# Order of a partial product, a GELU and two loads in the first two waves of an attention and MLP kernel

## The chip, the cores and the metric

The kernel runs on one core of a Trainium2 chip. The metric is the device time of one execution in microseconds; the median of several runs counts. Engines: PE (TensorE, matrix products), PEld (its weight loads), DVE (VectorE), ACT (ScalarE), POOL (GpSimd), and SP (SyncE), which here issues DMAs.

## The reference

The reference is a linear attention with decay per head, followed by an MLP with the quick GELU. Cut to what matters:

```python
q, k, v: (4, 8, 768, 64)   # batch, heads, sequence, head size; lam: (8,)
for b in range(12):                       # blocks of 64 positions
    intra = (qb @ kb.T) * Dmask           # lam ** (i - j) below the diagonal
    out[block] = intra @ vb + (qb * lam_pow) @ kv_state
    kv_state = lam**64 * kv_state + (kb * rev_pow).T @ vb
x = out as (3072 tokens, 512)
h = x @ w_in                              # 512 x 2048
y = (h * sigmoid(1.702 * h)) @ w_out      # 2048 x 512, result in float32
```

## The kernel before

The 3072 tokens are worked in six waves (0 to 5) of 512 tokens. Waves 0 and 1 take two batches each over 256 positions, in two halves c; waves 2 to 5 take 128 positions of all four batches. For each wave the kernel loads q, k and v, casts k and q to bf16 with their decay factors (`do_cast`), transposes them (`turn_pe` on PE, or `turn_dma` as a DMA transpose from SP, L248), multiplies scores (`d_scores` L262, `n_scores` L338), masks them, multiplies with v and the state, and writes the attention's result to `xT`. The MLP follows.

Products of both MLP layers are mostly made by a Strassen-like scheme of seven products on half blocks, numbered 1 to 7. Each product runs into a bank of PSUM (X, Q, V, in the first wave also W); some are copied out as a `part`, others are added to a part (`h_sb`, L604; `o_sb`, L488, L531). Products 5, 6, 7 and 3 use sums of the left side, products 4 to 7 differences of weights. The differences are made on DVE: `w_in_t` (L564) and `w_out_t` (`weight_sums`, L431), the sums `g_s` at L444, `x_s` at L577.

The tile framework runs in manual schedule: each engine executes its instructions in the order in which the code writes them, and semaphores are set from data and buffers. The order is hand written. For waves 1 to 5 it is a string of short steps (`STEPS`), each run by `one_step`: `a6` is product 6 of the first group of the first layer (with the copy or eviction of its bank; `v` at the end puts the copy on DVE, otherwise it is ACT, L224), `A5` the GELU behind product 5 of that group (`in_gelu`, L615), with b/B, c/C for the other groups; `P20` is product 2 of the second layer, half 0 (L464); `S`, `M`, `m` are scores and masks of the next wave, `v0` and `v1` the casts of v for it on ACT, `R` the rest of its attention; `gl`, `gh` are sums of the GELU's output, `L` loads, `i` differences of `w_in`, `X` the sums of x. The second wave (wave 1) has a head that is written out call by call ahead of `STEPS[1]`.

The second layer of wave 0 is `product0(n, m0, m1)`: steps m0 to m1 of the eight along the inner dimension of product n, for both halves of the tokens (two matmuls for each step). The weights `w_out` come in four chunks of four, so steps 0 to 2 use chunk 0, and 6 to 8 use chunk 3. POOL issues the loads of `w_in` and `w_out`; SP issues all loads of q, k and v but one, all DMA transposes and all stores. `leave0` evicts wave 0's banks; the stores wait in `late` and are issued where they are called.

Loads of wave 2 are split: `load(2, "kq")` stands in wave 0, `load(2, "v")` in the head of wave 1, between the two pairs of transposes of wave 2. `gate_pool` (L682) makes POOL wait for a sum of x before it casts the second k and q of wave 2. Stores, loads and transposes share SP's queue, in order. The tile of v has one buffer for each half.

Of the kernel before, what the change touches and what calls it, by code (L numbers as in the profile page):

```python
# [25 lines left out]
def kernel(  # L26
# [52 lines left out]
    def load_one(w, c, nm, src):  # L79
        x = ld.tile([P, H, 2 * D], f32, tag=f"{nm}{c}", bufs=LD_BUFS[nm], name=f"{nm}f")  # L80
        if w < ND:
            n = H if w or (nm == "v" and c) else H // 2
            for h in range(0, H, n):
                (nc.gpsimd if w == 0 and c and nm == "v" else nc.sync).dma_start(
                    out=x[:, h : h + n],
                    in_=src[2 * w + c, h : h + n, 0 : 2 * P, :].rearrange("h (s a) d -> s h (a d)", a=2))
        else:
            nc.sync.dma_start(out=x.rearrange("p h (a d) -> p (h a) d", a=2),
                              in_=src[2 * c : 2 * c + 2, :, w * P : (w + 1) * P, :].rearrange("b h s d -> s (b h) d"))
        loaded[w, c, nm] = x  # L90

    def load(w, nms="kqv"):
        src = {"k": k, "q": q, "v": v}
        if w < ND:
            for c in range(HF):
                for nm in nms:
                    if w or c == 0 or nm != "v":
                        load_one(w, c, nm, src[nm])
        else:
            for nm in nms:  # L100
                for c in range(HF):
                    load_one(w, c, nm, src[nm])
# [37 lines left out]
    def acc(name, dt=f32, shape=None, tag="a"):  # L140
        return ps.tile(shape or [P, 4, P], dt, tag=tag, bufs={"a": 5, "mm": 3}[tag], name=name)
# [104 lines left out]
    def turn_dma(w, c, nm):  # L246
        y = work.tile([P, 2 * NP, P], bf16, tag=f"{nm}T{c}", bufs={"k": 1, "q": 2}[nm], name=f"{nm}T")
        nc.sync.dma_start_transpose(out=y, in_=cast[w, c, nm].rearrange("p b c -> p (b c)"))  # L248
        trans[w, c, nm] = y
# [149 lines left out]
    def mlp1(w, fc):  # L399
        if w not in g_of:  # L400
            g_of[w] = gp.tile([P, FFC, W], bf16, tag="g", name="g_sb")
        j, i = w_in_of[fc]
        h = acc("ps_h", shape=[P, W], tag="mm")
        for kc in range(KC):
            nc.tensor.matmul(h, w_in_sb[j][:, kc, i * P : (i + 1) * P], xT[w][:, kc, :],
                             start=(kc == 0), stop=(kc == KC - 1))
        nc.scalar.activation(g_of[w][:, fc, :], h, GELU)
# [25 lines left out]
    def token_half(w, i, kh):  # L433
        return g_of[w].rearrange("p (m two) (i t) -> p two i m t", two=2, i=2)[:, kh, i]
# [11 lines left out]
    def w_half(m, kh, c):  # L446
        return w_out_sb[2 * m // CW][:, (2 * m) % CW + kh, c * 256 : (c + 1) * 256]
# [55 lines left out]
    def product0(n, m0, m1):  # L503
        if m0 == 0 and n in (1, 2, 7, 4):
            blocks[0, BANK0[n]] = acc(f"ps_{BANK0[n]}", shape=[P, 2, 256], tag="a" if n == 4 else "mm")
        bank = blocks[0, BANK0[n]]
        raw = [[token_half(0, i, kh) for kh in range(2)] for i in range(2)]
        x = {1: raw[0][0], 2: raw[0][1], 4: raw[1][1]}
        x = x[n] if n in x else half_sum[0][{5: 0, 6: 1, 7: 2, 3: 3}[n]]
        for t in range(2):  # L510
            for m in range(m0, m1):
                y = {1: (0, 0), 2: (1, 0), 3: (1, 1)}.get(n)
                y = w_half(m, *y) if y else TS[{4: 3, 5: 0, 6: 1, 7: 2}[n]][:, m]
                nc.tensor.matmul(bank[:, t], x[:, m, t * P : (t + 1) * P], y,  # L514
                                 start=(n in (1, 2, 7, 4) and t == 0 and m == 0),
                                 stop=(m == FFC // 2 - 1), skip_group_check=True)
# [62 lines left out]
    def in_product(w, g, n, tag, copy):  # L579
        if w not in g_of:  # L580
            g_of[w] = gp.tile([P, FFC, W], bf16, tag="g", name="g_sb")
        if isinstance(tag, dict):
            if n in (1, 2, 7):
                c = CHAIN[n]
                h_bank[w, g, c] = acc(f"ps_h{c}", shape=[P, 2, 256], tag=tag[c])
        elif n == 1:
            for c in tag[1:]:
                h_bank[w, g, c] = acc(f"ps_h{c}", shape=[P, 2, 256], tag={"a": "a", "m": "mm"}[tag[0]])
        bank, sums = h_bank[w, g, CHAIN[n]], x_sum.get(w)
        y = {1: (0, 0), 2: (0, 1), 4: (1, 1)}.get(n)  # L590
        y = x_half(w, *y) if y else sums[{5: 0, 6: 1, 7: 2, 3: 3}[n]]
        b = {1: (0, 0), 2: (1, 0), 3: (1, 1)}.get(n)
        for u in range(2):
            z = in_half(g, *b, u) if b else TI[g][{5: 0, 6: 1, 7: 2, 4: 3}[n]][:, :, u]
            for kc in range(2):
                nc.tensor.matmul(bank[:, u], z[:, kc], y[:, kc],  # L596
                                 start=(n in (1, 2, 7) and u + kc == 0), stop=(kc == 1), skip_group_check=True)
        if n in (1, 6, 7):
            h_part[w, g, n] = p = op.tile([P, 2, 256], f32, tag="part", bufs=6, name="part")
            copy(p, bank)  # L600
            return
        if n != 3:
            h = op.tile([P, 2, 256], f32, tag="o", name="h_sb")
            nc.vector.tensor_tensor(h, h_part[w, g, {2: 1, 5: 7, 4: 6}[n]], bank, op=ADD)  # L604
            bank = h
        if n == 3:
            in_gelu(w, g, n, bank)
        else:
            h_out[w, g, n] = bank
# [8 lines left out]
    def one_step(w, s):  # L618
        if s[0] == "+":
            w, s = w + 1, s[1:]  # L620
        x, a = w + 1, s[1:]
        if s[0] == "f":
            mlp1(w, int(a))
        elif s[0] in "abcd":
            k = "abcd".index(s[0])
            in_product(w, GR[w][k], int(s[1]), TAGS[w][k], dve_copy if s[2:] == "v" else act_copy)
        elif s[0] in "ABCD":
            in_gelu(w, GR[w]["ABCD".index(s[0])], int(a))
        elif s[0] == "i":
            in_sums(0, (int(a),))  # L630
        elif s[0] == "P":
            product(w, int(s[1]), (int(s[2]),))
        elif s[0] in "kq":
            do_cast(x, int(a), s[0], nc.vector)
        elif s[0] in "KQ":
            do_cast(x, int(a), s[0].lower(), nc.gpsimd)
        elif s[0] == "t":
            turn_dma(x, int(s[2]), s[1])
        elif s[0] == "v":
            cast_v(x, int(s[1]), ((act_copy, dve_copy)[s[2:] == "v"],))  # L640
        elif s[0] == "S":
            n_scores(x, int(a))
        elif s[0] == "M":
            n_masks(x, int(a))
        elif s[0] == "m":
            n_masks(x, int(a), True)
        elif s[0] == "R":
            n_rest(x)
        elif s[0] == "o":
            c11.pop(w)()  # L650
        elif s[0] == "X":
            x_sums(x)
        elif s[0] == "G":
            gate_pool(x_sum[w][3][0:1, 0, 0:1])
        elif s[0] == "g":
            m0, m1 = {"l": (0, 4), "h": (4, 8)}[s[1]]
            g_sums(w, m0, m1, tuple(int(c) - 1 for c in s[2:]))
        elif s[0] == "L":
            load(w + (1 if a == "w" else 2), "kq" if a == "k" else "v")
        else:  # L660
            raise ValueError(s)

    STEPS = {
# [17 lines left out]
    def gate_pool(x):  # L681
        nc.gpsimd.tensor_copy(behind_q, x)  # L682
# [4 lines left out]
    with tc.manual_schedule():  # L687
# [104 lines left out]
        product0(2, 4, 6)  # L792
        product0(4, 0, 4)
        product0(7, 4, 6)
        for n in (1, 2, 7):
            product0(n, 6, 8)
            if n != 2:
                leave0(n)
# [4 lines left out]
        cast_v(1, 0, (pool_copy, pool_copy))  # L803
        for nm in "kq":
            do_cast(1, 1, nm, nc.gpsimd)
        product0(4, 4, 8)
        leave0(4)
        leave0(2)
        turn_pe(1, 0, "k")
# [32 lines left out]
        for s in "A2 a7v c1".split():  # L842
            one_step(1, s)
        mlp1_half(1, 1, 4, 13)
        one_step(1, "B2")
        late[2]()
        late[5]()
        for nm in "kq":
            turn_dma(2, 0, nm)
        load(2, "v")  # L850
        gate_pool(x_sum[1][3][0:1, 0, 0:1])
        for nm in "kq":
            do_cast(2, 1, nm, nc.gpsimd)
            turn_dma(2, 1, nm)
        late[3]()
        late[4]()
        for s in STEPS[1].split():
# [34 lines left out]
```

## Time and profile before

| what | value |
|---|---|
| median of 3 runs | 194.1 us (193.7 to 194.93) |
| profiled execution, time | 194.76 us |
| profiled execution, span | 193.0 us |
| PE busy | 184.1 us, 95% of the span |
| DVE, ACT, POOL busy | 154.5, 130.2, 54.1 us |
| granted TensorE clock | 0.999 |
| HBM read and written | 27.26 and 6.29 MB |

The page of the profile gives busy times of one execution. The span starts with the first instruction and ends with the last; the execution's own time is 1.76 us more than the span. Times of single instructions come from the timeline of an engine: the start in us from the span's start, the duration, engine, line, operation, output and inputs, shapes, count, and in brackets the idle time before it with what ended that. Matmuls overlap, so for PE the distance between starts is the cost, not the duration shown: four matmuls of 128x256 start 0.44 us after the four before them.

### The profile page before, as it was taken

Reading aid. Unit: us, or ns where it says so; the run is one execution under the profiler, and the core shown is the slowest. Engines: PE = TensorE matmul, PEld = TensorE weight load, DVE = VectorE, ACT = ScalarE, POOL = GpSimd, SP = SyncE. Lnnn points to the kernel's source line nnn. Section 1 sums busy time; section 2 is a strip of 40 time slices with the busy share of each in tenths; the row PEclk is TensorE's granted clock in tenths of the full one; section 3 lists DMA queues with packets and bytes.
Section 4 is the critical chain, followed back from the end, with each engine's and each line's share of the span. In section 5 each row is a group of like instructions: output and inputs, shape, how many; then the busy total and the mean of one; then the engine's idle time right before and its main releaser. Section 6 shows DMA issues by size and latency. Waiting matters only on the chain.

```text
span 193.0 us, 5556 instructions
## 1 busy us (share of the span) xinstructions
PE 184.1 (95%) x2293; PEld 150.8 (78%) x2293; DVE 154.5 (80%) x296; ACT 130.2 (67%) x243; POOL 54.1 (28%) x79
## 2 busy tenths in 40 slices
PE   7689999899999899999999999999999999999993
PEld 2357646788787688888888888888888888888882
DVE  1796699877696899888799979799879797889950
ACT  4867664155868956469878388878388876597711
POOL 5488300039727000097000195000393000000000
PEclk9999999999999999999999999999999999999999
DMA  5999999999998989967799836999365903300113
GB/s 152 307 251 184 200 207 206 279 294 292 237 160 199 215 195 233 225 163 112 159 239 225 257 109 153 203 256 242 132 163 115 212 7 109 112 3 0 49 35 137
DMA packets 89599, 33.91 MB, mean 176 GB/s; under 512 B 67430, under 2 KB 89446, under 8 KB 89574
## 3 DMA queue, kind: packets, MB, share of 16 engines
q1 hardware_dynamic: 84676, 28.84, 61.6%
q0 software_dynamic: 4896, 4.72, 14.5%
q8 instruction: 18, 0.29, 0.7%
q14 instruction: 7, 0.06, 0.1%
q10 hardware_dynamic: 2, 0.00, 0.0%
HBM read 27.26 MB, written 6.29 MB: 174 GB/s over the span
## 4 chain that ended last, share of the span: by engine, by line
PE 72%; DMA 16%; POOL 5%; SPq 2%; DVE 2%; issue 0%; ACT 0%; POOLq 0%; DVEq 0%; ACTq 0%
PE ps_X L464 18%; PE ps_hX L596 15%; PE ps_V L464 9%; DMA w_out<-in_moe_w_out_dram 9%; PE ps_hV L596 7%; PE ps_Q L464 5%; PE ps_hQ L596 4%; DMA vf<-in_v_dram 3%; PE ps_X L514 3%; DMA qf<-in_q_dram 3%; PE ps_s L338 2%; PE ps_o L393 2%; DMA qT<-qs 2%; SPq L248 1%; POOL w_in L184 1%; PE ps_o L380 1%
## 5 line engine op out<-in xcount | busy, mean ns | idle before, releaser
L615 ACT ACTIVATE g_sb<-h_sb 128x512 bf16<-128x512 f32 x57 | 34.5, 631 | 1.7 <-DVE h_sb L604 1.7
L464 PEld LDWEIGHTS <-g_s 128*128 128x128 bf16 x320 | 30.9, 98 | 4.1
L596 PEld LDWEIGHTS <-w_in_t 128*128 128x128 bf16 x304 | 29.7, 98 | 4.1 <-issue 0.5
L224 ACT COPY part<-ps_hX 128x512 f32<-128x512 f32 x34 | 19.5, 587 | 10.5 <-PE ps_hX L596 10.3
L464 PEld LDWEIGHTS <-g_sb 128*128 128x128 bf16 x240 | 22.8, 98 | 3.4
L596 PEld LDWEIGHTS <-w_in 128*128 128x128 bf16 x228 | 22.1, 98 | 2.8
L596 PE MATMUL ps_hX<-x_s,w_in_t 128*128 128x256 bf16 x152 | 22.6, 272 | 0.4 <-ACT part L224 0.4
L444 DVE TENSOR_TENSOR g_s<-g_sb 128x1024 bf16<-128x1024 bf16 (+1 forms) x26 | 16.5, 646 | 5.6 <-ACT g_sb L615 5.6
L464 PE MATMUL ps_X<-w_out_t,g_s 128*128 128x256 bf16 x160 | 19.1, 273 | 0.0
L682 POOL CAST behind_q<-x_s 1x1 f32<-1x1 bf16 x4 | 0.7, 176 | 63.7 <-DVE x_s L577 63.7
L212 POOL TENSOR_TENSOR qs<-qf,q_pow 128x512 bf16<-128x512 f32 x16 | 16.3, 1041 | 1.1 <-DMA qf<-in_q_dram 1.1
L604 DVE TENSOR_TENSOR h_sb<-part,ps_hX 128x512 f32<-128x512 f32 x19 | 12.9, 681 | 4.5 <-PE ps_hX L596 4.5
L212 POOL TENSOR_TENSOR ks<-kf,k_pow 128x512 bf16<-128x512 f32 x16 | 16.3, 1040 | 0.1
L221 DVE COPY part<-ps_hV 128x512 f32<-128x512 f32 x18 | 12.4, 687 | 3.2 <-PE ps_hV L596 3.2
L604 DVE TENSOR_TENSOR h_sb<-part,ps_hV 128x512 f32<-128x512 f32 x19 | 13.0, 683 | 1.0 <-PE ps_hV L596 1.0
L604 DVE TENSOR_TENSOR h_sb<-part,ps_hQ 128x512 f32<-128x512 f32 x19 | 12.9, 680 | 0.4 <-PE ps_hQ L596 0.4
L615 ACT ACTIVATE g_sb<-ps_hX 128x512 bf16<-128x512 f32 x19 | 11.1, 589 | 1.9 <-PE ps_hX L596 1.9
L347 ACT ACTIVATE sm<-ps_s,inv_pow 128x512 bf16<-128x512 f32 x16 | 10.1, 688 | 3.1 <-PE ps_s L338 3.1
L224 ACT CAST v_sb<-vf 128x1024 bf16<-128x1024 f32 (+1 forms) x12 | 10.4, 905 | 1.5 <-DMA vf<-in_v_dram 1.5
L351 DVE SCALAR_TENSOR_TENSOR sm<-ps_s,inv_pow,mask 128x512 bf16<-128x512 f32 x16 | 11.2, 744 | 0.2 <-PE ps_s L338 0.2
L596 PE MATMUL ps_hQ<-xT,w_in 128*128 128x256 bf16 x76 | 11.4, 273 | 0.0
L596 PE MATMUL ps_hV<-xT,w_in_t 128*128 128x256 bf16 x76 | 11.4, 273 | 0.0
(128 smaller groups left out, 364.8 us busy)
## 6 DMA issues: line engine op xcount, KB each, us to landing
kf<-in_k_dram SPq DMA_DIRECT2D x10, 512.0 KB, 6.3
qf<-in_q_dram SPq DMA_DIRECT2D x10, 512.0 KB, 6.7
vf<-in_v_dram SPq DMA_DIRECT2D x10, 512.0 KB, 5.9
out_dram<-o_sb SPq DMA_DIRECT2D x24, 128.0 KB, 2.5
out_dram<-o_sb SPq DMA_DIRECT2D x12, 256.0 KB, 2.6
w_out<-in_moe_w_out_dram POOLq DMA_DIRECT2D x4, 512.0 KB, 13.6
kf<-in_k_dram SPq DMA_DIRECT2D x4, 256.0 KB, 3.1
qf<-in_q_dram SPq DMA_DIRECT2D x4, 256.0 KB, 5.2
```

The costliest lines, as they stand in the source:

```text
L212: eng.tensor_tensor(x.rearrange("p b (r i j d) -> p j (b r) i d", i=2, j=2, d=D)[:, j], f.rearrange("p h (a d) -> p (h a) d", a=2).rearran ...
L221: nc.vector.tensor_copy(out, in_)
L224: nc.scalar.copy(out, in_)
L338: nc.tensor.matmul(s2[h][:, b, :], kT[hs, (b % 2) * NP + p, :], qT[hs, (b % 2) * NP + p, :], start=True, stop=True)
L347: nc.scalar.activation(sm, s, COPY, scale=inv_pow[:, n : n + 1])
L351: nc.vector.scalar_tensor_tensor(sm, s, inv_pow[:, n : n + 1], mask.to_broadcast([P, B, P]), op0=MUL, op1=MUL)
L444: nc.vector.tensor_tensor(o, x, y, op=f)
L464: nc.tensor.matmul(bank[:, t], x[:, m, t * P : (t + 1) * P], y, start=(n in (1, 2, 7) and t == ts[0] * last and m == 0), stop=(m == FFC // ...
L514: nc.tensor.matmul(bank[:, t], x[:, m, t * P : (t + 1) * P], y, start=(n in (1, 2, 7, 4) and t == 0 and m == 0), stop=(m == FFC // 2 - 1), ...
L596: nc.tensor.matmul(bank[:, u], z[:, kc], y[:, kc], start=(n in (1, 2, 7) and u + kc == 0), stop=(kc == 1), skip_group_check=True)
L604: nc.vector.tensor_tensor(h, h_part[w, g, {2: 1, 5: 7, 4: 6}[n]], bank, op=ADD)
L615: nc.scalar.activation(g_of[w][:, a : b + 1 : b - a, 256 * i : 256 * i + 256], bank, GELU)
```

## The change

Three steps are moved; no instruction is added or taken away.

1. In wave 0, steps 4 to 6 of product 4 (four matmuls into bank W) are issued ahead of the steps that use the last chunk of `w_out`. The rest of product 4 is issued where it was, as steps 6 to 8.
2. In wave 1, the GELU `B2` moves from the head, where it stood ahead of the copies of `a6`, `b7` and `b6` on ACT, into `STEPS[1]` behind `b6`.
3. In wave 1, the two loads of v for wave 2 move on SP's queue from between the two pairs of DMA transposes to behind the second pair.

```diff
     STEPS = {
-        1: ("a6 b7 b6 a5 c2 b5 A5 c6 a4 c7v B5 b4 A4 c5 a3 C2 c4 B4 b3 c3 P10 C5 i0 gl3 i2 C4 P11 i1 gh3 S0 S1 M0 i3 P20 m1 "
+        1: ("a6 b7 b6 B2 a5 c2 b5 A5 c6 a4 c7v B5 b4 A4 c5 a3 C2 c4 B4 b3 c3 P10 C5 i0 gl3 i2 C4 P11 i1 gh3 S0 S1 M0 i3 P20 m1 "
...
         product0(4, 0, 4)
         product0(7, 4, 6)
+        product0(4, 4, 6)
         for n in (1, 2, 7):
             product0(n, 6, 8)
             if n != 2:
...
         for nm in "kq":
             do_cast(1, 1, nm, nc.gpsimd)
-        product0(4, 4, 8)
+        product0(4, 6, 8)
         leave0(4)
...
         mlp1_half(1, 1, 4, 13)
-        one_step(1, "B2")
         late[2]()
         late[5]()
         for nm in "kq":
             turn_dma(2, 0, nm)
-        load(2, "v")
         gate_pool(x_sum[1][3][0:1, 0, 0:1])
         for nm in "kq":
             do_cast(2, 1, nm, nc.gpsimd)
             turn_dma(2, 1, nm)
+        load(2, "v")
         late[3]()
```

## The prediction

> **What bounds the kernel now.** I read the page's busy shares first, then the chain that ended last, then the windows by stage, and last the timelines of single engines around each change.
>
> ```profile
> PE 184.1 (95%) x2293; PEld 150.8 (78%) x2293; DVE 154.5 (80%) x296; ACT 130.2 (67%) x243; POOL 54.1 (28%) x79
> ```
>
> PE is busy for 95% of the span, and in the chain that ended last every piece from 67.66 us to the last eviction is PE's. So whatever moves PE's start at 67.66 moves the end, and what counts before it is where PE stands still. The windows (columns: PE, PEld, DVE, ACT, POOL, granted clock, DMA share, GB/s) give the places.
>
> ```profile
> 30.00:36.30 6.30, 6.30 (x52) 4.90 (x50) 6.03 (x16) 1.65 (x3) 0.00 (x0) 1.00 1.21 247
> 36.30:40.80 4.50, 3.98 (x38) 3.51 (x37) 3.95 (x13) 1.76 (x3) 0.00 (x0) 1.00 0.87 244
> 40.80:54.00 13.20, 13.20 (x302) 10.91 (x299) 9.23 (x18) 9.36 (x18) 11.23 (x15) 1.00 1.10 279
> 54.00:66.50 12.50, 12.13 (x118) 10.09 (x112) 10.38 (x21) 10.04 (x20) 4.28 (x6) 1.00 1.07 190
> 66.50:80.70 14.20, 13.33 (x218) 11.46 (x218) 12.54 (x24) 8.90 (x16) 0.00 (x0) 1.00 0.95 222
> 80.73:108.79 28.06, 28.06 (x354) 24.52 (x353) 24.63 (x45) 20.92 (x38) 8.23 (x9) 1.00 0.86 191
> ```
>
> PE loses 0.52, 0.37 and 0.87 us in three of these stretches and nothing in a later wave (28.06 of 28.06). Each loss is one wait, and each of the three edits touches one of them. The timelines:
>
> ```profile
> 35.75 0.60 PE L514 MATMUL ps_V<-w_out_t,g_s 128*128 128x256 bf16 x4
> 36.87 0.60 PE L514 MATMUL ps_X<-w_out,g_sb 128*128 128x256 bf16 x4 [0.52 <-DMA w_out<-in_moe_w_out_dram]
> ...
> 58.23 0.60 PE L596 MATMUL ps_hX<-x_s,w_in_t 128*128 128x256 bf16 x4
> 59.20 0.60 PE L596 MATMUL ps_hX<-x_s,w_in_t 128*128 128x256 bf16 x4 [0.37 <-ACT part L224]
> ...
> 66.50 0.29 PE L338 MATMUL ps_s<-qT,kT 64*128 64x128 bf16 x4
> 67.66 0.51 PE L338 MATMUL ps_s<-qT,kT 64*128 64x128 bf16 x12 [0.87 <-DMA qT<-qs]
> ```
>
> The bracket is the idle time before the row and what ended it: the last chunk of w_out, ScalarE's copy of a bank, the transposed q.
>
> **Edit 1, the fourth product (W) of the first wave.** Four matmuls of chunk 2 move from behind the sixth product to ahead of the last chunk; nothing is added. Four matmuls of this form take 0.44 us (start to start, 36.87 to the next four at 37.30). They need the last of the four weight differences of chunk 2 on VectorE: the pair of L431 that starts at 35.48 and takes 0.89 ends at 36.37. So they start at about 36.41 and end their slot at 36.85, when the chunk lands (36.83). The group at 36.87 stays where it is, and the later W group shrinks from eight to four (its start is 39.92): PE is 0.44 us earlier at 40.80. Behind it: the transposes on PE need ks, done at 39.87 (38.45 + 1.42) against 40.36; the fifth product needs the bank that ScalarE's copy frees at 40.71 (40.12 + 0.59) against 40.80; the transposes of qs need 41.21 against 41.68; POOL's second ks is ready at 45.12 (42.79 + 2.33) against 46.04; POOL's second qs at 47.58 (45.08 + 2.50) against 47.65. POOL is tied to a load there and doesn't shift, so the last margin is the thinnest, 0.07. Bounds: 0 (all eaten there) to 0.44; I take 0.44, since every listed producer ends first.
>
> **Edit 2, a GELU (B2) behind two copies.** ScalarE runs B2 just ahead of the copy for which PE waits:
>
> ```profile
> 57.56 0.60 ACT L419 ACTIVATE g_sb<-ps_h 128x512 bf16<-128x512 f32 x1 [0.15 <-PE ps_h L417]
> 58.05 0.62 ACT L615 ACTIVATE g_sb<-h_sb 128x512 bf16<-128x512 f32 x1
> 58.57 0.58 ACT L224 COPY part<-ps_hX 128x512 f32<-128x512 f32 x1
> 59.04 0.60 ACT L224 COPY part<-ps_hV 128x512 f32<-128x512 f32 x1
> 59.52 0.61 ACT L224 COPY part<-ps_hX 128x512 f32<-128x512 f32 x1
> 60.61 0.63 ACT L615 ACTIVATE g_sb<-h_sb 128x512 bf16<-128x512 f32 x1 [0.49 <-DVE h_sb L604]
> ```
>
> The row at 58.05 is B2, the next three are the copies a6, b7, b6. B2 is now written behind b6, so all three rise by one slot: a6 starts at 58.05 (its matmuls, started at 57.36, are through at 57.96) and ends at 58.63. PE's group at 59.20 then starts at 58.70, close behind the group at 58.23 (58.67 by the pitch of 0.44): 0.50 gained. B2 falls into ScalarE's 0.49 idle ahead of 60.61 and is needed first by the product at 64.65, so it costs nothing; without this idle time, one slot of 0.52 would fall on the GELU at 60.61. VectorE had waited 1.91 us ahead of 59.89 and follows PE. The next bank, for the group at 60.18, waits for b6, now done at 59.62: the same 0.1 us of waiting as before. Bounds 0.3 to 0.53; I take 0.50.
>
> **Edit 3, loads of v behind the second pair of transposes.** SP's queue:
>
> ```profile
> 56.17 2.49 SPq L248 DMA_TRANSPOSE qT<-qs  x1
> 58.71 2.63 SPq L88 DMA_DIRECT2D vf<-in_v_dram  x2
> 61.51 3.07 SPq L248 DMA_TRANSPOSE kT<-ks  x1
> 64.67 1.26 SPq L248 DMA_TRANSPOSE qT<-qs  x1
> ```
>
> POOL finishes the second ks at 59.71 and qs at 61.73. kT could go at 59.8 but stands behind two loads until 61.51, is issued slowly (3.07, against 3.22 for two in wave three) and lands 5.1 us after its start, against 2.7 in wave three; qT goes at 64.67 and lands 2.94 later, at 67.61. After the change, with POOL's gate 0.44 earlier by edit 1, kT starts at 59.33 and is out of SP by 60.6 to 61.8 (1.26 to 2.49 us), qT at 61.3 to 61.9, landing 2.9 to 3.7 later (rows of this qT and of wave three): 64.2 to 65.6. PE gets there at 66.50 - 0.94 = 65.56 and needs it 0.14 later. The two sets of eight score matmuls take 1.60 us now (66.50 to 68.10) and 0.55 where nothing is late (71.70 to 72.25): 1.05 gained. Bounds: a loss of 0.5 to a gain of 1.05; I take 1.05, by the landing of the same qT.
>
> A rule of the Trainium skill bears on this ("DMA: Bandwidth & Descriptors", section Queues, rings and completion order): each DMA engine consumes descriptors in ring order, though completions need not come in that order. The 5.1 against 2.7 us agrees with the first half. By the rule the loads in front are the whole delay and the gain stands; if the order had no weight, only the 1.8 us of later issue would go, and the wait would still vanish.
>
> What waits now: the loads of v go at some 62.7 instead of 58.7, behind qT's cast. They landed 4.6 and 5.4 us after issue; so 67.3 and about 69, or with the slowest 512 KB load of this stretch (8.4) 71.1 and 71.7. ScalarE casts them at 71.47 and 73.57, 2 us earlier in the new clock: 69.5 and 71.6. The multiplication with v needs both at 74.4 (76.42 now), so cover is left. Behind v on SP stand four stores (66.03 now, about 65.4 then, nobody waits) and the loads of the next k and q (68.67), first wanted by POOL at 82.45. Further on PE is 1.99 us earlier; VectorE, which has no idle time between 68.04 and 77.5, begins that stretch only 1.2 us earlier (behind the g_s sum at 67.11). Its masks, due for PE at 75.85 and 76.9 in the old clock, end at 74.43 and 75.10, the sum for the sixth product at 73.11 where its second half starts at 74.45; its last eviction at 79.90 comes out even. Less than 0.05 is lost.
>
> **Sum.** 0.44 + 0.50 + 1.05 = 1.99, say 2.0 us with what is lost under the rounding. The profiled execution took 194.76 us, span 193.0; it would take 192.8, span 191.0. It stood 0.66 above the median of the runs, 194.1, so I forecast 192.1. A measurement of this kernel tells about 1% from no change, 1.94 us; the sum lies just beyond.
>
> **Rivals.**
> 1. qT is still late. For it: the first kT landed 4.7 us after issue, and qT behind it took 2.49 to issue. With kT's issue at 2.49 and qT's landing at 4.9, qT comes at 66.8 against 65.70: 1.1 us of stall, gain 0.9, 193.2. Against: no load or store stands close ahead of this pair any more.
> 2. Edit 1 gives nothing: its four matmuls wait for VectorE (0.06 of margin) or POOL's qs eats it at 47.65. Gain 1.55, 192.55; then part of the gain of edit 1 only moved to a new wait.
> 3. Slower: v is late. ScalarE works in order, so a late v0 holds the cast (1.05), the two masked evictions behind it (1.27) and VectorE's masks (0.75). The third head's output starts at about 76.9 in the old clock; the break-even is v0 at 76.9 - 3.1 = 73.8, or 11.1 us after issue at 62.7. Past it each us costs one: at 13 us, 1.9 lost, 196.0. For it: DMA share is 0.84 to 1.28 in the windows from 60 to 66, and the moved megabyte meets stores and loads. Against: the slowest load of 512 KB here took 8.4. The Trainium skill's overview ("Trainium Kernel Development and Optimization", Key Constraints) says that all issuing queues share the 16 DMA engines; the windows' high share agrees.
>
> **How the numbers follow.** Forecast 0.64, rival 1 0.15, rival 2 0.13, rival 3 0.08. The forecast's own range is 191.6 to 192.6; with rivals 1 and 2 and the spread of the median, 191.4 to 193.6; outside it lie rival 3 and a few hundredths each way. Faster by over 1% means below 192.16: three quarters of the forecast (0.48) and a little of rival 2 (0.02), 0.50; slower 0.08, rival 3; within 1% the other 0.42.
>
> **What would show it.** Right: no wait for w_out above 0.1 us ahead of the last chunk on PE; the group behind b6 follows within 0.45 us; kT and qT issued ahead of v and landing 2.7 to 3.7 after issue; the sixteen scores in about 0.55 us; wave three starting about 2 us earlier, with the same 28.06 us. Wrong: a wait of PE for qT, a POOL wait at the transposes near 47.6, or ScalarE idle ahead of the casts of v beyond 1.5 us.

## The result and the profile after

The median went from 194.1 us (7 runs, 193.59 to 194.93) to 192.53 us (7 runs, 192.03 to 193.26). The ratio is 0.9917, 95% interval 0.9892 to 0.9943: 1.6 us faster, against 2.0 forecast; the interval reaches from 1.1 to 2.1 us. The two profiled executions differ by the 2.0: span 193.0 to 191.0, time 194.76 to 192.68. That is in part luck, since the profiled execution of before stood 0.66 us above its median and that of after only 0.15. Ratios with their intervals are those on record for fast runs alone, and differ from the quotients of the medians by up to 0.3%, about 0.5 us.

The page's line of busy shares, and the windows with the same columns as before the change:

```profile
PE 185.2 (97%) x2291; PEld 151.9 (80%) x2293; DVE 154.1 (81%) x296; ACT 130.3 (68%) x243; POOL 54.2 (28%) x79
```

```profile
36.30:40.40 4.10, 3.97 (x37) 3.55 (x37) 3.88 (x12) 1.45 (x3) 0.00 (x0) 1.00 1.00 296
40.40:54.00 13.60, 13.60 (x305) 11.25 (x303) 9.80 (x18) 10.11 (x19) 11.16 (x15) 1.00 1.08 269
54.00:65.50 11.50, 11.50 (x103) 9.70 (x101) 9.94 (x20) 9.52 (x20) 4.35 (x6) 1.00 0.79 152
65.50:78.70 13.20, 13.20 (x218) 11.39 (x218) 12.36 (x25) 8.86 (x16) 0.00 (x0) 1.00 0.97 229
```

Between 36.3 us and the start of wave three, PE's 0.37 and 0.87 us of idle time are gone, and 0.13 of the 0.52 is left. PE's timeline at the three places, and ScalarE's and SP's:

```profile
35.66 0.60 PE L514 MATMUL ps_V<-w_out_t,g_s 128*128 128x256 bf16 x4
36.43 0.60 PE L514 MATMUL ps_W<-w_out_t,g_sb 128*128 128x256 bf16 x4 [0.17 <-DVE w_out_t L431]
36.87 0.60 PE L514 MATMUL ps_X<-w_out,g_sb 128*128 128x256 bf16 x4
...
57.79 1.05 PE L596 MATMUL ps_hX<-x_s,w_in_t 128*128 128x256 bf16 x8
58.67 0.60 PE L596 MATMUL ps_hQ<-xT,w_in 128*128 128x256 bf16 x4
...
65.54 0.62 PE L338 MATMUL ps_s<-qT,kT 64*128 64x128 bf16 x16
```

```profile
57.12 0.60 ACT L419 ACTIVATE g_sb<-ps_h 128x512 bf16<-128x512 f32 x1 [0.15 <-PE ps_h L417]
57.61 0.58 ACT L224 COPY part<-ps_hX 128x512 f32<-128x512 f32 x1
58.08 0.60 ACT L224 COPY part<-ps_hV 128x512 f32<-128x512 f32 x1
58.55 0.62 ACT L224 COPY part<-ps_hX 128x512 f32<-128x512 f32 x1
59.03 1.25 ACT L615 ACTIVATE g_sb<-h_sb 128x512 bf16<-128x512 f32 x2
```

```profile
56.07 1.81 SPq L248 DMA_TRANSPOSE qT<-qs  x1
59.29 1.23 SPq L248 DMA_TRANSPOSE kT<-ks  x1
61.30 1.24 SPq L248 DMA_TRANSPOSE qT<-qs  x1
62.60 2.54 SPq L88 DMA_DIRECT2D vf<-in_v_dram  x2
```

The W group stands ahead of the last chunk; the two groups that had ScalarE's copy between them run as one row of eight; the sixteen score matmuls are one row, without a wait; kT and qT are issued ahead of v, as soon as POOL is done.

These two traces alone do not settle which edit brought what. Two theories are set against each other. Theory L: as long as the loads of v stand between the pairs of transposes, the landing of the second qT is a deadline that PE's work does not move, so edits 1 and 2 only make PE wait longer there. Its rival, theory A: the three terms add up, as the prediction wrote them.

### The profile page after: what moved, and what is told of

It is laid out like the page before. It is cut to its first block, busy times and chain, and to the rows that moved or that the text cites. A ratio compares the mean times of both kernels' runs of the same rounds, so it can differ in the third digit from the quotient of the medians.

```text
span 191.0 us, 5553 instructions
## 1 busy us (share of the span) xinstructions
PE 185.2 (97%) x2291; PEld 151.9 (80%) x2293; DVE 154.1 (81%) x296; ACT 130.3 (68%) x243; POOL 54.2 (28%) x79
## 3 DMA queue, kind: packets, MB, share of 16 engines
q0 software_dynamic: 4896, 4.72, 14.8%
## 4 chain that ended last, share of the span: by engine, by line
PE 79%; DMA 12%; DVE 4%; POOL 2%; SPq 1%; issue 0%; ACT 0%; ACTq 0%
PE ps_X L464 19%; PE ps_hX L596 18%; PE ps_V L464 9%; PE ps_hV L596 9%; DMA w_out<-in_moe_w_out_dram 6%; PE ps_Q L464 5%; PE ps_hQ L596 4%; DMA vf<-in_v_dram 3%; PE ps_X L514 3%; DMA qf<-in_q_dram 3%; DVE w_out_t L431 2%; PE ps_s L338 2%; PE ps_o L393 2%; PE ps_h L417 2%; DVE g_s L444 2%; POOL w_in L184 1%
## 5 line engine op out<-in xcount | busy, mean ns | idle before, releaser
L596 PE MATMUL ps_hV<-x_s,w_in_t 128*128 128x256 bf16 x76 | 11.4, 273 | 0.0
```

Of the source, the lines that this page charges most:

```text
L596: nc.tensor.matmul(bank[:, u], z[:, kc], y[:, kc], start=(n in (1, 2, 7) and u + kc == 0), stop=(kc == 1), skip_group_check=True)
```

## The experiments

**One edit at a time.** The diffs are parts of the change's own. First edit 1 alone:

> Edit 1 alone (four matmuls of product 4 ahead of the last chunk of w_out), the other two as before. Theory L: as long as the loads of v stand between the pairs, the second qT lands at about 67.6 us whatever PE does, because SP's queue is not moved by PE; PE then comes 0.44 earlier to the scores and waits 0.44 longer there (about 1.3 instead of 0.87), and the time is that of before, gain 0 to 0.1 us. Rival A, the three terms add up: gain 0.44 us, the wait for qT stays at 0.87.

Edit 2 alone:

> Edit 2 alone (the GELU B2 behind the copies). Theory L: the wait of PE for ScalarE's copy near 59.2 us goes (0.37 to 0), PE reaches the scores at 66.0, and the wait for qT grows from 0.87 to about 1.4; gain 0 to 0.1 us. Rival A: gain 0.50 us with the wait for qT unchanged.

Edit 3 alone:

> Edit 3 alone (loads of v behind the second pair of transposes). Theory L and rival A agree on about 1.05 us gained (kT issued at 59.8, qT at 61.8 and landed by 64.5, before PE comes at 66.5), the waits of 0.52 for w_out and 0.37 for the copy stay. Rival B, qT is still late for another reason: gain under 0.5 us and a wait of PE for qT left.

Edits 1 and 2 without edit 3:

> Edits 1 and 2 without edit 3. Theory L: PE reaches the scores at 65.56 and waits there for qT until about 67.6, 1.8 us of idle time shown; gain 0 to 0.15 us. Rival A: gain 0.94 us, a wait of 0.87. With the kernel of the change (gain 1.6 by the runs, 2.0 by the profiles) this also gives the worth of edit 3 on top of the others: 1.9 by L, 1.05 by A.

Measured, against before (median 194.12 on the same chip):

| kernel | median us | ratio, 95% interval | PE's wait for qT | span, us | PE's second group of scores starts |
|---|---|---|---|---|---|
| before (as shown) | 194.12 | | 0.87 | 193.0 | 67.66 |
| edit 1 | 193.85 | 1.0012, 0.9982 to 1.0042 | 0.46 | 191.9 | 66.62 |
| edit 2 | 193.61 | 1.0001, 0.9971 to 1.0030 | 1.84 | 192.5 | 67.20 |
| edits 1, 2 | 193.77 | 0.9998, 0.9968 to 1.0028 | 0.94 | 191.6 | 66.23 |
| edit 3 | 193.03 | 0.9956, 0.9931 to 0.9982 | none | 191.1 | |

Rows of PE's timeline from the kernels with edit 1, with edit 2, and with both, in this order:

```profile
66.62 0.51 PE L338 MATMUL ps_s<-qT,kT 64*128 64x128 bf16 x12 [0.46 <-DMA qT<-qs]
```

```profile
67.20 0.51 PE L338 MATMUL ps_s<-qT,kT 64*128 64x128 bf16 x12 [1.84 <-DMA qT<-qs]
```

```profile
66.23 0.51 PE L338 MATMUL ps_s<-qT,kT 64*128 64x128 bf16 x12 [0.94 <-DMA qT<-qs]
```

None of the three ratios without edit 3 shows a gain. A's 0.44, 0.50 and 0.94 us would be ratios of 0.9977, 0.9974 and 0.9952; the first and the last lie outside their intervals, the second inside. By medians the three kernels are 0.27, 0.51 and 0.35 us below before, so the noise is as large as the terms. The times do not prove L either: if edit 1 is worth nothing by itself, as the next experiments show, A leaves only 0.50 us for both edits, and 0.9974 lies inside the interval of edits 1 and 2 too.

What speaks for L is the traces. In all four profiles with v in front PE waits for qT. SP's rows follow each other there with gaps under 0.2 us from about 31 us on, where SP had waited for a load of w_out, up to this qT. POOL had the ks for the second kT ready 1.4 to 2.3 us before SP issued it. So the queue sets qT's landing, not PE. The last two columns show that the end follows it: span less start of that row is 125.3 to 125.4 us in all four, however early PE had come. So what edits 1 and 2 save in such an execution is waited away.

The waits expected by L were off (0.46, 1.84 and 0.94 us against 1.3, 1.4 and 1.8), because the deadline differs between executions: the second kT was issued at 61.51, 60.81, 61.09 and 60.17 us in these four. Executions of one kernel differ too: SP issued its second load of k for wave 2 at 44.77 and at 44.07 in the two profiles of the kernel with all three edits. So a wait in one profile is not a term of the kernel, only of that execution. Edit 3 alone gains 0.85 us by the ratio, with the interval of 0.35 to 1.3 around the 1.05 forecast for that term. What edit 3 adds behind the other two is 1.1 or 1.6 us by the ratios (0.9941 or 0.9917 against 0.9998), between the 1.05 of A and the 1.9 of L; it does not decide.

**Two edits at a time.** These ask what edits 1 and 2 are worth once qT is no deadline. Theory M, in the first expectation, says that edit 1 is worth little because the wait that it removes is not there in every execution. Without edit 1:

> Edits 2 and 3 without edit 1. Theory M: the wait for the last chunk of w_out differs between executions (0.52 us in the profile of before, 0.31 with edit 2, none with edit 3, where the chunk came before PE wanted it), so edit 1 is worth only 0 to 0.2 us on top: this kernel lies within 0.2 us of the one with all three, about 1.4 us under before, and shows a wait for w_out of 0 to 0.5. Rival: edit 1 is worth its whole 0.44 us, and this kernel is 0.4 slower than the one with all three.

Without edit 2:

> Edits 1 and 3 without edit 2. Edit 2 is worth 0.50 us once qT is no longer the deadline: this kernel shows PE's wait of 0.37 for ScalarE's copy and is 0.5 us slower than the one with all three. If edit 2's gain were absorbed further on (by VectorE, by the casts of v), the two would be equal, with a wait of PE somewhere between 60 and 80 us in the kernel with all three.

The three together, once more for comparison:

> All three edits, beside the kernels of two edits on the same chip. 1.4 to 1.7 us under before; edits23 0 to 0.2 slower by theory M and 0.4 by its rival; edits13 0.5 slower.

And edit 2 half done:

```diff
-        1: ("a6 b7 b6 B2 a5 c2 b5 ...
+        1: ("a6 B2 b7 b6 a5 c2 b5 ...
```

> All three edits, but B2 stands behind the first copy only (a6 B2 b7 b6). Working of the prediction: PE's group behind the first copy follows at once (no wait of 0.37), but the copy b6 comes one slot (0.5) later, and the group that needs its bank, the third after it, waits 0.5 to 0.6 instead of 0.1; so the gain of edit 2 is lost again, 0.5 us slower than with all three. Rival: only the first copy mattered, and the time is that of all three.

Against before (193.51 on that chip): all three 192.38 us (0.9941, 0.9911 to 0.9971), edits 2 and 3 192.33 (0.9951, 0.9918 to 0.9985), edits 1 and 3 193.07 (0.9960, 0.9927 to 0.9992), B2 in the middle 192.67 (0.9950, 0.9921 to 0.9978). By medians, leaving out edit 1 costs nothing (0.05 us less) and leaving out edit 2 costs 0.69 us, where 0.5 was expected; each is known to some 0.5 us, so the times alone leave open whether edit 1 brings its 0.44. The traces say more on both. The wait of 0.37 us for ScalarE's copy is in all four profiles without edit 2, and in none of those with it (in the kernel with B2 in the middle another comes in its place). For edit 1, PE at the last chunk, first without it (edits 2 and 3), then with it (all three):

```profile
35.00 0.60 PE L514 MATMUL ps_V<-w_out_t,g_s 128*128 128x256 bf16 x4
35.59 0.60 PE L514 MATMUL ps_X<-w_out,g_sb 128*128 128x256 bf16 x4
```

```profile
34.96 0.60 PE L514 MATMUL ps_V<-w_out_t,g_s 128*128 128x256 bf16 x4
35.89 0.60 PE L514 MATMUL ps_W<-w_out_t,g_sb 128*128 128x256 bf16 x4 [0.34 <-DVE w_out_t L431]
36.33 0.60 PE L514 MATMUL ps_X<-w_out,g_sb 128*128 128x256 bf16 x4
```

From the start of V to the start of X it takes 0.59 us without edit 1; with the 0.44 for the four W matmuls that come later, 1.03. With edit 1 it takes 1.37 in this pair. Over all executions profiled for this study the first kind gives 1.56 (before), 1.35, 0.87 and 1.03, mean 1.20; the second 1.21 (after), 1.19, 1.37, 1.34, 1.37, 1.16, 0.88, 0.88, 1.39 and 0.87, mean 1.17. Edit 1 replaces a wait for the DMA, 0 to 0.68 us in start distances, by a wait for VectorE's last weight difference, 0 to 0.52. The two rows of VectorE in the profile of before show both deadlines, the difference that the W matmuls need (ready at 36.37) and the last chunk (landed just ahead of 36.85):

```profile
35.48 0.89 DVE L431 TENSOR_TENSOR w_out_t<-w_out,w_out_t 128x512 bf16<-128x512 bf16 x2
36.85 0.76 DVE L431 TENSOR_TENSOR w_out_t<-w_out 128x512 bf16<-128x512 bf16 x2 [0.48 <-DMA w_out<-in_moe_w_out_dram]
```

The means differ by 0.03 us, but four and ten values that scatter this much fix that only to some 0.4. Both deadlines stand in every trace (the chunk's is the issue of its load plus the load's time to landing), so the order that was not run can be worked out for each execution. Without edit 1, X starts 0.44 after V or when the chunk lands, whichever is later, and four W matmuls follow; with it, W starts 0.44 after V or when the difference is ready, and X starts 0.44 later or when the chunk lands. With the small lags seen in before (0.03 and 0.04 us), this rule gives the start of X on record within 0.03 us in all fourteen profiles. By this estimate edit 1 gains from -0.39 to 0.46 us, mean 0.01, known to some 0.14. The 0.46, the highest of the fourteen, is the execution of before that the prediction was made from. Theory M holds, and A's 0.44 for edit 1 does not.

With B2 in the middle, PE's wait has moved by two groups:

```profile
58.72 0.60 PE L596 MATMUL ps_hQ<-xT,w_in 128*128 128x256 bf16 x4
59.78 0.92 PE L596 MATMUL ps_hX<-x_s,w_in_t 128*128 128x256 bf16 x7 [0.46 <-ACT part L224]
```

The group behind the first copy follows at once, and the one that needs b6's bank waits 0.46, as expected. So both copies matter in the trace, and B2 belongs behind b6. The time rose by 0.3 us in the median, where 0.5 was expected; that is inside the noise.

**Where v stands.** All with edits 1 and 2. One load between the pairs and one behind:

```diff
             turn_dma(2, 0, nm)
+        load_one(2, 0, "v", v)
...
             turn_dma(2, 1, nm)
-        load(2, "v")
+        load_one(2, 1, "v", v)
```

> All three edits, but only one of the two loads of v (512 KB) is behind the second pair; the other stays between the pairs. Working of the prediction: with one load in front SP is free again by 59.3, so kT is still issued as soon as POOL is done; its descriptors stand behind 512 KB instead of 1 MB, it lands 3 to 4 us after issue instead of 2.7, qT by 64.5 to 65.5, just in time: time as with all three within 0.3 us, no wait of PE for qT above 0.2. Rival: any load in front costs its whole share, half of the 1.05 to 1.9 us comes back as a wait for qT, 0.5 to 0.9 us slower.

Both ahead of the first pair:

```diff
         late[5]()
+        load(2, "v")
         for nm in "kq":
             turn_dma(2, 0, nm)
```

> All three edits, but both loads of v stand ahead of the first pair of transposes instead of behind the second. If the order on SP's queue is what counts, the first pair is issued 2.7 us later and slowly, the second kT cannot go before 62.5 and qT lands at 67.5 to 68.5; PE waits 2 to 3 us for it, and the time is that of before or up to 1 us over it. Rival: the loads were only in the way where they ran beside the second pair; ahead of the first pair they are done by 61, and the time is that of all three within 0.4 us.

Both behind the four stores (`load(2, "v")` behind `late[4]()`):

> All three edits, and the loads of v behind the four stores too. They are issued at about 65.3 instead of 62.6 and land at 70 and 71.5. By the break-even of the prediction's third rival, 71.8 in the new clock (73.8 less 2.0), ScalarE's first cast may be that late at no cost: ScalarE idles about 0.5 to 1 us ahead of it, the time is that of all three within 0.3 us. Rival: the casts have no slack in a stretch where ScalarE and VectorE work in order, and each us of the cast's delay costs one: 0.5 to 1 us slower.

Both behind the next k and q (in `STEPS[1]`, `Lk` becomes `Lk Lw`):

> All three edits, and the loads of v behind the stores and the next k and q. Issued at about 73, landed at 78 to 79. By the third rival's rule each us past 71.8 costs one: ScalarE waits for v from 69.5 on, PE loses 6 to 7 us between 72 and 82 us, the time is 6 to 7 us over that of all three and 4.5 to 5.5 over before. Rival: much less (under 3), if PE finds other work in the meantime or the loads come sooner.

Against before (193.5): one load in front 192.13 us (0.9930, 0.9897 to 0.9963); both ahead of the first pair 193.19 (0.9983, 0.9955 to 1.0010); behind the stores 192.41 (0.9974, 0.9936 to 1.0012); behind k and q 201.93 (1.0446, 1.0388 to 1.0504).

One load in front shows no cost. SP's rows of that kernel show kT issued when POOL is done with ks, at 58.64:

```profile
57.51 0.58 SPq L88 DMA_DIRECT2D vf<-in_v_dram  x1
58.64 2.30 SPq L248 DMA_TRANSPOSE kT<-ks  x1
61.04 1.25 SPq L248 DMA_TRANSPOSE qT<-qs  x1
```

This kT landed 4.4 us after issue, against 4.8 to 5.1 behind two loads and 2.7 behind none. More bytes in front mean a later landing; that agrees with the ring order of the Trainium skill ("DMA: Bandwidth & Descriptors", section Queues, rings and completion order). Loads that move at the same time as the transpose and slow it would look alike, and no run here tells the two apart. qT landed 3.0 after issue, at 64.04, and PE came at 64.89. Only what goes past PE's arrival costs.

Both ahead of the first pair: qT was issued at 63.86 and landed 2.8 later, at 66.7, sooner than the 67.5 expected. The median is 0.8 over that of all three (on another chip) and 1.1 over that of one load in front (on the same chip), so most of the gain is lost. The expected wait of PE is not in the profile, because this execution is not a typical one. It is the slowest of the ten (194.26 us), and PE was late in it: after a wait of 1.31 us that ended at 14.65, the granted clock was 0.50 from 15 to 18 us, and PE came to the scores only at 67.11. In the five other profiles of kernels with all three edits and no wait for b6's copy it came at 64.89 to 65.97, which would leave a wait of some 0.6 to 1.7 us for a qT that lands at 66.7. By this estimate the late qT accounts for the loss; no trace shows it.

Behind the stores: ScalarE waits for v, and PE doesn't.

```profile
70.32 1.05 ACT L224 CAST v_sb<-vf 128x1024 bf16<-128x1024 f32 x1 [0.33 <-DMA vf<-in_v_dram]
71.28 1.26 ACT L347 ACTIVATE sm<-ps_s,inv_pow 128x512 bf16<-128x512 f32 x2
73.20 1.04 ACT L224 CAST v_sb<-vf 128x1024 bf16<-128x1024 f32 x1 [0.66 <-DMA vf<-in_v_dram]
```

The second cast ends at 74.24, and PE starts the product with v at 74.84: 0.6 us of cover are left. The first cast, at 70.32, is ahead of the 71.8 of the rule, and no time is lost, as the rule says. The ratio's interval reaches from a whole gain to none, so the time itself tells little: two of the ten runs took 194.4 and 194.5 us at a granted clock of 0.99, the other eight 192.0 to 193.2. The trace decides here.

Behind k and q the rival comes true, at a higher price than expected (8.4 us over before, 9.5 over all three by medians, 6 to 7 expected):

```profile
80.70 0.64 PE L380 MATMUL ps_o<-qT,kv 64*64 64x128 bf16 x15 [6.11 <-ACT sm L347]
82.29 1.71 PE L393 MATMUL ps_o<-sm,v_sb 128*64 128x128 bf16 x28 [0.60 <-ACT v_sb L224]
84.78 2.54 PE L464 MATMUL ps_X<-w_out_t,g_s 128*128 128x256 bf16 x16
```

```profile
78.00:80.00 2.00, 0.00 (x0) 0.00 (x0) 0.00 (x0) 0.99 (x2) 0.00 (x0) 0.81 1.11 252
80.00:82.00 2.00, 1.00 (x19) 0.58 (x18) 1.17 (x3) 2.00 (x4) 0.00 (x0) 0.50 0.12 27
82.00:84.00 2.00, 1.71 (x36) 1.71 (x38) 2.00 (x4) 1.97 (x5) 0.00 (x0) 0.50 0.21 50
84.00:86.00 2.00, 2.00 (x38) 1.60 (x35) 1.62 (x5) 0.81 (x2) 0.00 (x0) 0.50 0.39 95
86.00:88.00 2.00, 2.00 (x20) 1.77 (x18) 0.76 (x3) 0.15 (x1) 0.00 (x0) 0.98 0.53 126
```

The cast started at 79.01, when v came; 7.2 past the 71.8 of the rule. PE idles 6.11 + 0.60 = 6.7. The rest is clock: PE stopped at 74.6 and started the next wave at 87.16, and in between the granted clock (the value behind POOL's) is 1.00 in the windows up to 78 us, then 0.81, then 0.50 until 86. From the first row of this stretch (74.13) to the next wave it took 13.03 us, against 3.85 in the profile after (73.84 to 77.69): 9.18 lost, of which 2.5 are left for the work at half clock.

## Why the prediction was right, point by point

- **What bounds.** Right: PE is the chain, the three waits were its only ones between 36.3 and 80 us, and the later waves kept 28.1 us. Span and execution came out at 191.0 and 192.68, against 191.0 and 192.8.
- **Edit 1.** The place was right (36.43, 36.87, then 40.36 instead of 40.80), and PE took qs at 47.65 without a wait. The margin of 0.07 for POOL was not put to the test: POOL is tied to a load there, which came earlier in this execution, and its qs was ready at 47.21. The size failed: 0.44 came from one execution, the one of fourteen in which the edit is worth most, and the mean is 0.01 to 0.03. The prediction had the number for this in hand: the row of VectorE's last difference, ready only at 36.37, is a second deadline that the edit puts in the chunk's place. Its second rival named that deadline and priced edit 1 at nothing: 192.55 us, against 192.53 measured. The median measured lies nearer to that rival than to the 192.1 forecast, though it is not known well enough to choose between them by itself. The term has about the size of the miss, 0.4 between the 2.0 forecast and the 1.6 measured, though the interval of the result would still hold the whole 2.0.
- **Edit 2.** Right in the trace: a6's copy from 57.61, no wait, B2 in ScalarE's idle slot, 0.1 left ahead of b5's bank (58.67 to 59.22). The 0.50 is the trace's, and the wait that it removes is the same 0.37 in all four profiles without edit 2; by runs the edit is worth 0.7 us, known to some 0.5.
- **Edit 3.** Right: kT at 59.29 (59.33 forecast), qT at 61.30, landing 2.7 us after issue, at 64.0 (64.2 to 65.6 forecast), 1.5 us ahead of PE; the 16 scores took 0.55 us (65.54 to 66.09). The size of 1.05 is again one execution's: the wait for qT was 0.46 to 1.84 us in the four profiles with v in front.
- **The sum.** It came out near the measured time, but not for its own reasons alone. The prediction added three terms as if each stood alone. One of them is worth about nothing on average, and the traces show that the other saving ahead of qT is waited away as long as the third wait stands. All three edits were made together, so this second flaw cost nothing. The first rival (qT still late) would have taken both savings along, and priced only part of that.
- **VectorE and v as cover.** Right: masks and sums kept up; v0's cast began at 69.46 without a wait (69.5 forecast). Two readings there were off, and nothing hung on them: the 5.4 us given for the landing of the second load of v is the median of the two, which took 4.6 and 6.2; and the high DMA share, taken as agreement with engines that all queues share, shows only that they were busy.

No kernel here clearly beats the one with all three: edits 2 and 3 (192.33) and one load in front (192.13) lie inside its noise. Edits 2 and 3 without edit 1 did as well.

## What to carry to other kernels

Waits in a row on one engine do not add up as gains: find which of them is a deadline set by another queue, since everything saved ahead of it is waited away until it goes. Before a wait in one profile becomes a term of a sum, ask whether its releaser (here a DMA) comes at the same time in other executions, and which producer becomes the next deadline for the work put in its place. A load may stand ahead of a transpose as long as the transpose still lands before its reader comes; what counts is the slack at the reader.

## What the runs showed of the hardware

A pause of PE of 6.1 us cost more than itself: the granted clock fell to 0.50 and stayed there until about 86, more than 5 us after the work had begun again at 80.70. The Trainium skill ("TensorE: Matmul & The Clock Gate", Part 1: The HAM clock gate) says that an idle window of about 3.4 us halves the clock and that sustained work brings it back; the trace agrees on the half clock.

A shorter pause can be followed by it too. In the execution profiled with both loads of v ahead of the first pair, PE waited 1.31 us, up to 14.65, and the granted clock was 0.91 from 14 to 15 us, 0.50 from 15 to 18 and 0.89 from 18 to 19. The pause is shorter than the window that the page gives. Yet pauses of 1.84 us (edit 2 alone, ahead of 67.20) and 1.16 us (B2 in the middle, ahead of 14.05) left the clock at 1.00. So the length of one pause does not decide it, and what else does is not shown here. If the clock was either 1.00 or 0.50 at each moment, the windows give an estimate of how long the half clock held: 14.8 to 18.2 and 79.2 to 86.0, or 3.4 and 6.8 us.

Issuing the second kT on SP took 1.23 us in the profiles with no load of v close ahead of it and 2.30 to 3.07 behind one or two of them; the first kT took 3.75 behind two, and 1.36 to 2.49 behind stores. So what stands in front in the queue goes with a longer hold on SP itself as well as a later landing.
